# Attention keys in three full chunks and a shared rest, in a fused attention and SwiGLU kernel

## The chip, the cores and the metric

The kernel runs on one core of a Trainium2 chip. The metric is device time in microseconds (us), lower is better. The kernel before takes 453.81 us (median of three runs, 453.68 to 455.35). In the profiled execution the span from the first to the last instruction is 451.7 us, with a mean granted TensorE clock of 0.998. "PE" is TensorE, "PEld" its weight loads, "DVE" VectorE, "ACT" ScalarE, "POOL" GpSimd, "SP" SyncE.

## What is computed

Softmax attention over 8 batches and 12 heads, 448 tokens, head size 64; its output, with the heads side by side, is the input of a SwiGLU block with widths 768, 1536 and 768.

```python
batch, n_heads, seq, head_dim = (8, 12, 448, 64)
scores = scale * np.matmul(q, k.transpose(0, 1, 3, 2))
attn = softmax(scores)                       # over the keys
attn_out = np.matmul(attn, v)
x = attn_out.transpose(0, 2, 1, 3).reshape(3584, 768)
g = x @ w_gate                               # 768 x 1536
val = x @ w_val                              # 768 x 1536
return (silu(g) * val) @ w_out               # 1536 x 768
```

(Shortened: the reference subtracts the row maximum before the exponential; the names are its own.)

## The kernel before

The heads are worked in 48 pairs. For each pair the keys stand as four chunks of 112. `qk` computes the scores of one chunk for both heads (two matmuls, each on 64 rows of the array) and ScalarE takes their exponential into E. PV multiplies E with V and a column of ones (65 columns), and VectorE closes the pair: a reciprocal of the sums and a multiplication. The result is transposed into X. The FFN takes X in blocks of 384 or 512 tokens. Its first part has twelve steps per block: a gate group of six matmuls (gp), a value group of six (vp), tanh on ScalarE (sg), and two operations on VectorE (t, hts). Its second part has output steps of twelve matmuls (op), each copied by ScalarE to osb and sent out.

```python
ps_s = ctx.enter_context(tc.tile_pool(name="ps_s", bufs=3, space=PSUM))   # [128, 2, 512] each
ps_f = ctx.enter_context(tc.tile_pool(name="ps_f", bufs=2, space=PSUM))   # one bank each
...
def qk(pr, c):
    s = ps_s.tile([128, 2, 512], FP32, tag="s")
    for hx in range(2):
        nc.tensor.matmul(s[:, hx, 0:S], lhsT=t[ts(hx, 64), c * P : c * P + 128], rhs=..., ...)
    nc.scalar.activation(e[:, :, 0:S], s[0:P, :, 0:S], AF.Exp, scale=sm_scale)
...
def pv_chunk(pr, c):
    if c == 0:
        accs[pr] = ps_f.tile([128, 512], FP32, tag="f", name="acc")
    ...                                      # 8 matmuls of 65 columns, both heads in one bank
    nc.vector.reciprocal(r[:, 0:7], a7[:, :, D])
    nc.vector.tensor_tensor(xt[:, 0:n], a7[:, 0:n, 0:D], r[...], ALU.mult)
...
def ffn1_steps(kk, c0, n, hts):
    for fb in range(NFB):
        ...
        gp = ps_s.tile([128, 2, 512], FP32, tag="s", name="gp")[:, 0]     # or a ps_f tile
        group("g", gp)
        nc.scalar.activation(sg[:, 0:n], gp[:, 0:n], AF.Tanh, scale=0.5)
        vp = ps_f.tile([128, 512], FP32, tag="f", name="vp")
        group("v", vp)
        nc.vector.scalar_tensor_tensor(t1[:, 0:n], sg[:, 0:n], 1.0, gp[:, 0:n], ALU.add, ALU.mult)
        nc.vector.scalar_tensor_tensor(hts[:, fb, 0:n], t1[:, 0:n], 0.5 * HS, vp[:, 0:n], ...)
        yield
...
def ffn2_steps(...):
        op = ps_f.tile([128, 512], FP32, tag="f")
        for fb in range(NFB):
            nc.tensor.matmul(op[:, 0:w], lhsT=hts[:, fb, ts(ch, 128)], rhs=wo[oh][...], ...)
        nc.scalar.activation(osb[:, ds(m0, w)], op[:, 0:w], AF.Copy, scale=1.0 / HS)
        ...                                  # DMA to out
```

The order is fixed by the program. After an opening of attention alone it goes in visits: two or three score chunks of later pairs, the PV of a ripe pair if there is one (a visit without is called bare), then steps of the FFN.

Of the kernel before, what the change touches and what calls it, by code (L numbers as in the profile page):

```python
# [26 lines left out]
NX = 6  # L27
NV = 5
VS = 9
EB = 15  # L30
# [3 lines left out]
def kernel(  # L34
# [24 lines left out]
    MQ = S - D  # L59
# [13 lines left out]
    load_table("exp_and_others")  # L73

# [7 lines left out]
    ps_f = ctx.enter_context(tc.tile_pool(name="ps_f", bufs=2, space=PSUM))  # L82

    Es = [consts.tile([P, NC * EB + 1, D], FP16, name=f"E{i}") for i in range(NE)]
    Xts = [consts.tile([128, 7, D], FP16, name=f"xt{i}") for i in range(NX)]
    Xrs = [consts.tile([D, 128], FP16, name=f"xr{i}") for i in range(3)]
    Vts = [consts.tile([P, 2, NC, D + 2], FP16, name=f"vo{i}") for i in range(NV)]
    vraw = consts.tile([P, VS, 2, NC, D], FP16, name="vraw")
# [17 lines left out]
    def dummy(n):  # L106
        wp = ps_f.tile([128, 512], FP32, tag="f", name="wp")
        for _ in range(n):
            nc.tensor.matmul(wp[:], lhsT=warm[:, 0:128], rhs=warm[:], start=True, stop=True)  # L109

    def load_qk32(pr):
        rq = raws.tile([P, 2, NC, D], FP32, tag="rq", bufs=RB)
        rk = raws.tile([P, 2, NC, D], FP32, tag="rk", bufs=RB)
        for dst, src in ((rq, q), (rk, k)):
            nc.sync.dma_start(dst[:], src[0, 2 * pr : 2 * pr + 2].rearrange("h (p c) d -> p h (c d)", c=NC))
        raw[pr] = (rq[:], rk[:])
# [3 lines left out]
    def load_qk16(pr, n=2):  # L120
        h0 = 2 * (pr % 2) if pr >= 14 else 0
        if h0 == 0:
            q16 = raws.tile([P, 4, NC, D], FP16, tag="rq", bufs=RB, name="q16")
            k16 = raws.tile([P, 4, NC, D], FP16, tag="rk", bufs=RB, name="k16")
            pairbuf[:] = [q16, k16]
        q16, k16 = pairbuf
        for dst, src in ((q16, q), (k16, k)):
            flat = src.rearrange("b h s d -> (b h) s d")[2 * pr : 2 * pr + 2 * n]
            nc.gpsimd.dma_start(dst[:, ds(h0, 2 * n)], flat.rearrange("h (p c) d -> p h (c d)", c=NC))  # L129
        for i in range(n):  # L130
            h = h0 + 2 * i
            raw[pr + i] = (q16[:, h : h + 2], k16[:, h : h + 2])

    def load_v(pr, n=1):
        b, h = divmod(2 * pr, H)
        nc.gpsimd.dma_start(  # L136
            vraw[:, ds(pr % VS, n)].rearrange("p r h c d -> p (r h) (c d)"),
            v[b, h : h + 2 * n].rearrange("h (p c) d -> p h (c d)", c=NC),
        )
# [17 lines left out]
    def prep(pr):  # L157
        rq, rk = raw[pr]
        if pr == 0 or pr >= NPE:
            qk16 = attp.tile([P, 2, NC, 2, D], FP16, tag="qk16", bufs=3)  # L160
            for t, src in enumerate((rq, rk)):
                dst = qk16[:, 1 - t].rearrange("p c h d -> p h c d")
                if pr == 0:
                    nc.vector.tensor_copy(dst[:, 0], src[:, 0])
                    nc.scalar.activation(dst[:, 1], src[:, 1], AF.Copy)
                else:
                    nc.gpsimd.tensor_copy(dst, src)  # L167
        qkT[pr] = attp.tile([128, 2 * S + D], FP16, tag="qkT", name="qkT", bufs=5)
        if pr >= NPE:
            nc.sync.dma_start_transpose(  # L170
                qkT[pr][:, 0 : 2 * S].rearrange("p (c q) -> p c q", q=P),
                qk16[:].rearrange("p t c h d -> p (t c h d)"),
            )
            nc.sync.dma_start_transpose(
                qkT[pr][:, 2 * S :].rearrange("p (c q) -> p c q", c=1),
                qk16[0:D, 1, 0].rearrange("p h d -> p (h d)"),
            )
            return None

        def turn0():  # L180
            for t in range(2):
                tp = ps_s.tile([128, 2, 512], FP32, tag="s", name="tp")
                for c in range(NC):
                    for hx in range(2):
                        nc.tensor.matmul(
                            tp[ts(hx, 64), c // 2, ds(c % 2 * P, P)],
                            lhsT=qk16[:, 1 - t, c, hx],
                            rhs=ident[0:P, 0:P],
                            start=True,
                            stop=True,  # L190
                        )
                dst = qkT[pr][:, ts(1 - t, S)].rearrange("p (a x) -> p a x", a=2)
                nc.vector.tensor_copy(dst[:, 0], tp[:, 0, 0 : 2 * P])
                nc.scalar.activation(dst[:, 1], tp[:, 1, 0 : 2 * P], AF.Copy)
                if t == 0:
                    tq = tp
            nc.vector.tensor_copy(qkT[pr][:, 2 * S :], tq[:, 0, 0:D])

        def turn():
            if pr < FIRST + 2:  # L200
                tp = ps_s.tile([128, 2, 1024], FP16, tag="s", name="tp")[:, 0]
            else:
                tp = ps_f.tile([128, 1024], FP16, tag="f", name="tp")
            for i in range(2 * NC + 1):
                t, c = (1 - i // NC, i % NC) if i < 2 * NC else (0, 0)
                for hx in range(2):
                    src = raw[pr][t][:, hx, c, :]
                    nc.tensor.transpose(tp[ts(hx, 64), ts(i, P)], src, ident[0:P, 0:P])  # L208
            nc.vector.tensor_copy(qkT[pr][:], tp[:, 0 : 2 * S + D])  # L209
# [3 lines left out]
    def qk(pr, c):  # L213
        t = qkT[pr]
        s = ps_s.tile([128, 2, 512], FP32, tag="s")
        for hx in range(2):
            nc.tensor.matmul(  # L217
                s[:, hx, 0:S],
                lhsT=t[ts(hx, 64), c * P : c * P + 128],
                rhs=t[ts(hx, 64), ds(S + (1 - hx) * D, S)],  # L220
                start=True,
                stop=True,
            )
        e = Es[pr % NE][:, ds(c * EB, 16)].rearrange("p (h b) x -> p h (b x)", h=2)
        nc.scalar.activation(e[:, :, 0:S], s[0:P, :, 0:S], AF.Exp, scale=sm_scale)  # L225

    def qk_half(pr, half, between=None):
        for c in (2 * half, 2 * half + 1):
            qk(pr, c)
            if between and c % 2 == 0:  # L230
                between()
# [3 lines left out]
    def pv_chunk(pr, c):  # L235
        if c == 0:
            accs[pr] = ps_f.tile([128, 512], FP32, tag="f", name="acc")
        e = Es[pr % NE]
        vo = Vts[pr % NV]
        a7 = accs[pr][:, 0 : 7 * (D + 1)].rearrange("p (s d) -> p s d", s=7)  # L240
        for j in range(3):
            for hx in range(2):
                nc.tensor.matmul(  # L243
                    a7[:, 2 * j + hx],
                    lhsT=e[:, ds(c * EB + 9 * hx + 2 * j, 2)].rearrange("p b x -> p (b x)"),
                    rhs=vo[:, hx, c, 0 : D + 1],
                    start=c + j + hx == 0,
                    stop=False,
                )
        for hx in range(2):  # L250
            nc.tensor.matmul(  # L251
                a7[:, 6],
                lhsT=e[:, ds(c * EB + 6 + hx, 2)].rearrange("p b x -> p (b x)"),
                rhs=vo[:, hx, c, 0 : D + 1],
                start=False,
                stop=c == NC - 1 and hx == 1,
            )
        if c < NC - 1:
            return
        r = attp.tile([128, 8], FP32, tag="R", bufs=2, name="R")  # L260
        xt = Xts[pr % NX]
        nc.vector.reciprocal(r[:, 0:7], a7[:, :, D])  # L262
        n = 7 if pr < XPE else 6
        nc.vector.tensor_tensor(  # L264
            xt[:, 0:n],
            a7[:, 0:n, 0:D],
            r[:, 0:n].unsqueeze(2).to_broadcast([128, n, D]),
            ALU.mult,
        )
        if pr < XPE:  # L270
            return
        for hx in range(2):
            nc.vector.tensor_scalar(
                Xrs[pr % 3][:, ts(hx, D)], a7[ts(hx, D), 6, 0:D], r[ts(hx, D), 6:7], None, ALU.mult
            )

    def pv(pr):
        for c in range(NC):
            pv_chunk(pr, c)

    def turn_x(pr):
# [5 lines left out]
        xt = Xts[pr % NX]  # L287
        if pr < XPE:
            tp = accs[pr] if pr < FIRST else ps_f.tile([128, 512], FP32, tag="f", name="xtp")
            for j in range(3):  # L290
                nc.tensor.matmul(  # L291
                    tp[:, ts(j, 128)],
                    lhsT=xt[:, 2 * j : 2 * j + 2].rearrange("p h d -> p (h d)"),
                    rhs=ident[:],
# [3 lines left out]
            nc.vector.tensor_copy(dst[:, 0:MQ], tp[:, 0:MQ])  # L298
            return
        nc.sync.dma_start_transpose(  # L300
            dst[:, 0:MQ].rearrange("p (j q) -> p j q", j=3),
            xt[:, 0:6].rearrange("p j d -> p (j d)"),
        )
        nc.sync.dma_start_transpose(dst[:, MQ:S].rearrange("p (j q) -> p j q", j=1), Xrs[pr % 3][:])

    def turn_rests(b):
        tp = ps_f.tile([128, NHP, D], FP32, tag="f", name="rtp")
# [334 lines left out]
```

The softmax here doesn't subtract the row's maximum and nothing guards it: scores larger than these inputs give would overflow.

## Time and profile before

| what | before |
|---|---|
| time, median of 3 | 453.81 us |
| span of the profiled execution | 451.7 us |
| VectorE, ScalarE, POOL busy | 45%, 53%, 31% |
| exponentials | 192, mean 919 ns |
| first gate group of the FFN starts | 29.79 us |
| last score and PV work | before 386 us, then FFN alone |

A busy share is an average over stages. Matmuls are pipelined and the ends that the profile gives them are modelled, so a rate is read from the distance of two starts. In a line of the timeline the columns are start, length, engine, source line, operation, out<-in, shape and count; in brackets stands the idle time of that engine ahead of it and what ended it.

### The profile page before, as it was taken

What the parts mean: (1) busy time and instruction counts of PE and PEld (TensorE: products, weight loads), DVE (VectorE), ACT (ScalarE), POOL (GpSimd) and SP (SyncE); (2) the same over time, 40 slices, a digit from 0 to 9 for tenths busy, and PEclk for the clock granted to TensorE, in tenths of its full rate; (3) what the DMA queues carried; (4) which work ended last, traced back from release to release, by engine and by line L of the source; (5) the groups of instructions that cost most, each with busy time, mean ns of one, the idle gap of its engine ahead of it and who ended that gap; (6) DMA issues with size and microseconds to landing.
All of it is one profiled execution on the core that took longest, in us unless ns stands there. A gap on an engine that the chain in (4) does not pass through costs nothing.

```text
span 451.7 us, 9871 instructions
## 1 busy us (share of the span) xinstructions
PE 441.9 (98%) x4024; PEld 247.0 (55%) x4024; DVE 201.6 (45%) x447; ACT 238.8 (53%) x350; POOL 141.8 (31%) x228
## 2 busy tenths in 40 slices
PE   8999999999999999999999999999999999999995
PEld 3655565545455556454555656545455666544563
DVE  3666562456654434455443534353453544055300
ACT  6965666566746465554554546644555462222221
POOL 8755715927642225252313405330100000000000
PEclk9999999999999999999999999999999999999999
DMA  9999999999969379874749758772503112200033
GB/s 142 173 200 201 196 172 174 180 209 119 145 93 133 46 129 124 132 120 71 126 74 120 98 78 143 118 105 68 101 20 68 46 46 57 70 2 0 17 100 95
DMA packets 105101, 48.71 MB, mean 108 GB/s; under 512 B 59744, under 2 KB 101600, under 8 KB 105056
## 3 DMA queue, kind: packets, MB, share of 16 engines
q0 software_dynamic: 43392, 23.37, 41.2%
q1 hardware_dynamic: 61664, 24.71, 28.9%
q8 instruction: 31, 0.51, 0.5%
q14 instruction: 14, 0.11, 0.1%
HBM read 47.19 MB, written 11.01 MB: 129 GB/s over the span
## 4 chain that ended last, share of the span: by engine, by line
PE 93%; DVE 3%; ACT 2%; issue 1%; DVEq 0%; ACTq 0%
PE op L371 24%; PE gp L326 23%; PE vp L326 23%; PE s L217 9%; PE acc L243 9%; PE acc L251 2%; ACT E L225 2%; PE tp L208 1%; PE wp L109 1%; DVE t L345 1%; ACT sg L341 1%; DVE qkT L209 0%; DVE xt L264 0%; PE acc L291 0%; DVE hts L348 0%
## 5 line engine op out<-in xcount | busy, mean ns | idle before, releaser
L225 ACT ACTIVATE E<-s 112x896 f16<-112x896 f32 x192 | 162.1, 919 | 27.5 <-PE s L217 27.4
L326 PE MATMUL gp<-X,wg 128*128 128x384 f16 (+1 forms) x576 | 124.7, 352 | 0.0
L326 PE MATMUL vp<-X,wv 128*128 128x384 f16 (+1 forms) x576 | 124.6, 352 | 0.0
L371 PE MATMUL op<-wo,hts 128*128 128x384 f16 (+1 forms) x684 | 116.1, 323 | 0.0
L345 DVE SCALAR_TENSOR_TENSOR t<-sg,gp 128x384 f32<-128x384 f32 (+1 forms) x96 | 59.7, 621 | 121.8 <-ACT sg L341 121.8
L341 ACT ACTIVATE sg<-gp 128x384 f32<-128x384 f32 (+1 forms) x96 | 52.5, 547 | 84.8 <-PE gp L326 83.6
L371 PEld LDWEIGHTS <-hts 128*128 128x128 f16 x684 | 65.5, 98 | 45.9 <-issue 3.9
L326 PEld LDWEIGHTS <-wv 128*128 128x128 f16 x576 | 56.3, 98 | 52.6
L326 PEld LDWEIGHTS <-wg 128*128 128x128 f16 x576 | 53.1, 97 | 45.6 <-issue 1.1
L378 ACT ACTIVATE osb<-op 128x384 f32<-128x384 f32 (+1 forms) x57 | 27.8, 487 | 92.5 <-PE op L371 92.5
L167 POOL COPY qk<-q 112x512 f16<-112x512 f16 x37 | 22.9, 619 | 144.5 <-DMA qkT<-qk 143.1
L348 DVE SCALAR_TENSOR_TENSOR hts<-t,vp 128x384 f16<-128x384 f32 (+1 forms) x96 | 59.6, 621 | 10.0
L243 PEld LDWEIGHTS <-E 112*128 112x128 f16 x1152 | 46.7, 97 | 18.2 <-issue 17.5
L243 PE MATMUL acc<-vo,E 112*128 112x65 f16 x1152 | 53.0, 193 | 1.3 <-DVE vo L142 0.7
L217 PE MATMUL s<-qkT 64*128 64x448 f16 x384 | 50.6, 355 | 0.2
L251 PE MATMUL acc<-vo,E 112*128 112x65 f16 x384 | 42.9, 193 | 0.0
L262 DVE RECIPROCAL R<-acc 128x7 f32<-128x7 f32 x48 | 9.8, 205 | 70.6 <-PE acc L251 70.5
L129 POOL DMA_DIRECT2D k<-in_k_dram x44 | 29.0, 660 | 9.5 <-DMA wo<-in_moe_w_out_dram 7.8
L129 POOL DMA_DIRECT2D q<-in_q_dram x44 | 29.3, 666 | 5.2 <-PE s L217 2.5
L136 POOL DMA_DIRECT2D vraw<-in_v_dram x42 | 28.0, 666 | 8.4 <-DVE vo L142 7.2
L217 PEld LDWEIGHTS <-qkT 64*128 64x128 f16 x384 | 14.5, 94 | 25.8 <-issue 18.6
L264 DVE TENSOR_TENSOR xt<-acc,R 128x384 f16<-128x384 f32 (+1 forms) x48 | 27.6, 574 | 1.7
(41 smaller groups left out, 148.2 us busy)
## 6 DMA issues: line engine op xcount, KB each, us to landing
q<-in_q_dram POOLq DMA_DIRECT2D x41, 112.0 KB, 4.0
k<-in_k_dram POOLq DMA_DIRECT2D x41, 112.0 KB, 4.6
vraw<-in_v_dram POOLq DMA_DIRECT2D x39, 112.0 KB, 4.6
wg<-in_moe_w_gate_dram POOLq DMA_DIRECT2D x8, 288.0 KB, 10.1
wv<-in_moe_w_val_dram POOLq DMA_DIRECT2D x8, 288.0 KB, 10.2
wo<-in_moe_w_out_dram POOLq DMA_DIRECT2D x2, 1152.0 KB, 22.0
out_dram<-osb SPq DMA_DIRECT2D x8, 288.0 KB, 3.0
out_dram<-osb SPq DMA_DIRECT2D x8, 240.0 KB, 3.1
```

Source lines behind the costliest of these rows:

```text
L129: nc.gpsimd.dma_start(dst[:, ds(h0, 2 * n)], flat.rearrange("h (p c) d -> p h (c d)", c=NC))
L136: nc.gpsimd.dma_start(vraw[:, ds(pr % VS, n)].rearrange("p r h c d -> p (r h) (c d)"), v[b, h : h + 2 * n].rearrange("h (p c) d -> p h (c ...
L217: nc.tensor.matmul(s[:, hx, 0:S], lhsT=t[ts(hx, 64), c * P : c * P + 128], rhs=t[ts(hx, 64), ds(S + (1 - hx) * D, S)], start=True, stop=True,)
L225: nc.scalar.activation(e[:, :, 0:S], s[0:P, :, 0:S], AF.Exp, scale=sm_scale)
L243: nc.tensor.matmul(a7[:, 2 * j + hx], lhsT=e[:, ds(c * EB + 9 * hx + 2 * j, 2)].rearrange("p b x -> p (b x)"), rhs=vo[:, hx, c, 0 : D + 1] ...
L251: nc.tensor.matmul(a7[:, 6], lhsT=e[:, ds(c * EB + 6 + hx, 2)].rearrange("p b x -> p (b x)"), rhs=vo[:, hx, c, 0 : D + 1], start=False, st ...
L326: nc.tensor.matmul(dst[:, 0:n], lhsT=wslice(kind, fb, cb), rhs=X[kk][:, cb, ds(c0, n)], start=(cb == 0), stop=(cb == NCB - 1),)
L341: nc.scalar.activation(sg[:, 0:n], gp[:, 0:n], AF.Tanh, scale=0.5)
L345: nc.vector.scalar_tensor_tensor(t1[:, 0:n], sg[:, 0:n], 1.0, gp[:, 0:n], ALU.add, ALU.mult)
L348: nc.vector.scalar_tensor_tensor(hts[:, fb, 0:n], t1[:, 0:n], 0.5 * HS, vp[:, 0:n], ALU.mult, ALU.mult)
L371: nc.tensor.matmul(op[:, 0:w], lhsT=hts[:, fb, ts(ch, 128)], rhs=wo[oh][:, fb, ds(m0 - oh * OH, w)], start=(fb == 0), stop=(fb == NFB - 1),)
L378: nc.scalar.activation(osb[:, ds(m0, w)], op[:, 0:w], AF.Copy, scale=1.0 / HS)
```

## The change

Keys are split into three chunks of 128 and a rest of 64 instead of four chunks of 112. The rests of the four heads of two neighbouring pairs share one score tile: four matmuls on 64x64 quarters of the array, and one exponential. This is meant to fill the array's and ScalarE's 128 lanes. Keys of pairs up to 10 are loaded with seven tokens per partition and split by transposes on TensorE. V, and the keys of later pairs, are loaded in two halves of 64 partitions that share a token row. Each head's PV now has a PSUM bank of its own. The PSUM pool of two tiles becomes one tile F with two banks, and a helper hands out its halves in turn. The mix of FFN steps in a visit is planned anew so that a visit, where it can, ends with an output step. Some loads move (wo later, pair 0's q on ScalarE's queue).

```diff
+    ps_f = ctx.enter_context(tc.tile_pool(name="ps_f", bufs=1, space=PSUM))
+    F = ps_f.tile([128, 2, 512], FP32, name="F")
+    fturn = [0]
+
+    def fbank():
+        fturn[0] ^= 1
+        return F[:, 1 - fturn[0]]
...
+    def load_keys(eng, dst, src, h0, n):
+        for s in range(2):
+            rows = bass.AP(
+                src.tensor, (h0 * S + s * KR) * D, [[(2 * NC - 1) * D, 64], [S * D, n], [1, NC * D]]
+            )
+            eng.dma_start(dst[ts(s, 64)], rows)
...
     def qk(pr, c):
-        t = qkT[pr]
         s = ps_s.tile([128, 2, 512], FP32, tag="s")
+        if c < KR:
+            t = qkT[pr]
             for hx in range(2):
                 nc.tensor.matmul(
+                    s[:, hx, 0:S],
+                    lhsT=t[ts(hx, 64), ts(c + low(pr, hx), 128)],
...
+        else:
+            for hx in range(2):
+                for p in (pr, pr + 1):
+                    lo = low(p, hx)
+                    t = qkT[p]
+                    nc.tensor.matmul(
+                        s[ts(1 - lo, 64), hx, 0:S],
+                        lhsT=t[ts(hx, 64), ds(0 if lo else KR * 128 + 64, 64)],
...
+    def pv_open(pr):
+        if pr not in accs:
+            accs[pr] = ([F[:, 0], F[:, 1]] if pr < FIRST else [fbank(), fbank()], [0, 0])
...
+    def pv_close(pr):
+        ...
         for hx in range(2):
+            a4 = accs[pr][0][hx][:, 0 : (KR + 1) * (D + 1)].rearrange("p (s d) -> p s d", s=KR + 1)
+            nc.vector.reciprocal(r[:], a4[:, :, D])
+            nc.vector.tensor_tensor(xt[:, :, hx], a4[:, :, 0:D], r[...], ALU.mult)
...
             if gate_small[0]:
-                gp = ps_f.tile([128, 512], FP32, tag="f", name="gp")
+                gp = fbank()
...
-            vp = ps_f.tile([128, 512], FP32, tag="f", name="vp")
+            vp = fbank()
...
-                op = ps_f.tile([128, 512], FP32, tag="f")
+                op = fbank()
...
+            no = [int(x + y + 1 < len(plan) and bool(plan[x + y + 1][1])) for y in range(visits)]
...
+                for _ in range(nf):
+                    run_fv()
                 for _ in range(no):
                     run_o()
```

(Cut to its core; the diff as a whole also changes the opening's order and the layout of E, V and the transposes.)

## The prediction

> **What bounds the kernel now.** I read the page's busy shares and its chain first, then the costliest groups, then the timeline of one steady visit and of the tail.
>
> ```profile
> PE 441.9 (98%) x4024; PEld 247.0 (55%) x4024; DVE 201.6 (45%) x447; ACT 238.8 (53%) x350; POOL 141.8 (31%) x228
> PE 93%; DVE 3%; ACT 2%; issue 1%; DVEq 0%; ACTq 0%
> L371 PE MATMUL op<-wo,hts 128*128 128x384 f16 (+1 forms) x684 | 116.1, 323 | 0.0
> L378 ACT ACTIVATE osb<-op 128x384 f32<-128x384 f32 (+1 forms) x57 | 27.8, 487 | 92.5 <-PE op L371 92.5
> L264 DVE TENSOR_TENSOR xt<-acc,R 128x384 f16<-128x384 f32 (+1 forms) x48 | 27.6, 574 | 1.7
> ```
>
> TensorE is the bound: busy 98%, 93% of the chain, and its output step (op) waits for nothing. ScalarE's copy of that step waits 92.5 us for TensorE, never the reverse. What hides the copies shows in the timeline of one visit:
>
> ```profile
> 142.44 0.74 PE L217 MATMUL s<-qkT 64*128 64x448 f16 x6
> 142.84 2.53 ACT L225 ACTIVATE E<-s 112x896 f16<-112x896 f32 x3 [0.78 <-PE s L217]
> 143.11 0.36 PE L243 MATMUL acc<-vo,E 112*128 112x65 f16 x6
> ...
> 144.09 1.14 PE L326 MATMUL gp<-X,wg 128*128 128x384 f16 x6
> 144.29 0.20 DVE L262 RECIPROCAL R<-acc 128x7 f32<-128x7 f32 x1 [0.78 <-PE acc L251]
> ...
> 147.01 1.14 PE L326 MATMUL vp<-X,wv 128*128 128x384 f16 x6
> 147.21 0.49 ACT L341 ACTIVATE sg<-gp 128x384 f32<-128x384 f32 x1 [1.46 <-PE gp L326]
> 147.74 0.56 DVE L345 SCALAR_TENSOR_TENSOR t<-sg,gp 128x384 f32<-128x384 f32 x1 [0.73 <-ACT sg L341]
> ...
> 147.99 2.11 PE L371 MATMUL op<-wo,hts 128*128 128x384 f16 x12
> ...
> 148.40 0.56 DVE L348 SCALAR_TENSOR_TENSOR hts<-t,vp 128x384 f16<-128x384 f32 x1
> ...
> 150.03 0.74 PE L217 MATMUL s<-qkT 64*128 64x448 f16 x6
> 150.14 0.49 ACT L378 ACTIVATE osb<-op 128x384 f32<-128x384 f32 x1 [2.43 <-PE op L371]
> ```
>
> Steps between starts give TensorE's rates: gate or value group 0.975 us (1.295 at 512 columns, from 423.62 to 424.91 in the tail), output step 1.95, a PV matmul 0.030 (32 of them from 143.11 to 144.09), a score chunk 0.19 (three in 0.67, less 0.10). About 0.1 us is lost on entering the scores and again on leaving them. The value group ends at 147.985 and the output step starts at 147.99, although hts reads that value bank until 148.96. It can, because the two have different tiles. The tail shows the same without attention, a copy (0.49) every 1.9 to 2.0 us behind steps of 1.95:
>
> ```profile
> 438.76 0.49 ACT L378 ACTIVATE osb<-op 128x384 f32<-128x384 f32 x1 [1.41 <-PE op L371]
> 440.76 0.49 ACT L378 ACTIVATE osb<-op 128x384 f32<-128x384 f32 x1 [1.51 <-PE op L371]
> 442.66 0.49 ACT L378 ACTIVATE osb<-op 128x384 f32<-128x384 f32 x1 [1.41 <-PE op L371]
> ```
>
> **What the Trainium skill says.** "TensorE: Matmul & The Clock Gate", Part 3, says row and column tiles of the array run together. The trace agrees: two 448-column score matmuls cost 0.19 us[...]. "TensorEngine Tiling (Array Packing)", Key Properties, says that changing the mode drains the array; those are the two losses of 0.1. "PSUM — Partial Sum Buffer", the section on bank collisions, asks for guards by bank and quadrant: an engine reading one bank does not forbid TensorE another. The lines at 147.99 and 148.40 agree. "Perfetto Trace Analysis", Optimization Strategy, takes one repeated gap on the engine that should be saturated as a sign of too few PSUM buffers; the kernel before has none in the steady part, but I expect them after.
>
> **What the change saves.** (1) Scores: 192 chunks become 144 chunks and 24 shared rests. If four 64x64 tiles run together, a rest is 0.19 too: 24 x 0.19 = 4.5 us. (2) PV: still 1,536 matmuls, but 384 of them use half the rows in pairs: 192 x 0.030 = 5.7 us. (3) Mode changes: counted in the two instruction orders, 172 become 185, +1.3. Pure TensorE work, summed at these rates with the unchanged FFN (327 us), transposes and 2.6 of warm-up, goes from 436.0 to 427.1 us. (4) In the opening ScalarE is the limit: 26 exponentials before the first FFN group become 23, and 0.84 us each (2.53/3) makes 2.5 us. Before, TensorE starts at 1.2 and loses some 9 us to waits, 5.6 of them ahead of its first FFN group at 29.79; its matmuls end near 446.5.
>
> **What it adds: waits.** This decides my number. PSUM for accumulators, value groups, output steps and X transposes was a pool of two tiles. Now it is one tile F of two banks, from which a helper hands out alternate halves. In the built changed program the semaphore values show each user of F waiting for the reader of the *previous* user, although that reads the other bank:
>
> ```
> PE op -> F at 512: waits Activation >= 314, set by the copy of the op just before, at F offset 0
> PE op -> F at 0:   waits Activation >= 315, set by the copy of the op just before, at F offset 512
> ```
>
> In the program before, the same step waits for the copy of two steps earlier. So dependences are kept for F as a whole: two banks, but a depth of one. I counted these waits in the built program and priced each kind. Latencies from the visit: PE stream end to ACT or DVE 0.20 us; ACT to DVE 0.03; t end to hts 0.10; back to PE about 0.06 (the one short wait in the opening: xt ends 29.56, TensorE starts 29.61).
>
> - Output step after output step, 17 times: 0.20 + 0.49 (copy) + 0.06 = 0.75. Sum 12.6 (the last piece is shorter).
> - Output step after a value group, 40 times: hts must end. Counted from the gate group's end at 384: tanh to 0.69, t to 1.28, hts from 1.39 to 1.95, TensorE 2.01; the value group took 0.975 of it, so 1.04 is lost; 1.09 at 512 columns (operations of 0.60, 0.69, 0.69). In six bare visits (no PV, the gate in F) t also waits for the value group: 1.46 or 1.74. Sum 18 x 1.04 + 16 x 1.09 + 3 x 1.46 + 3 x 1.74 = 45.8.
> - Value group after PV, 42 times: both heads' close must end. 0.20, two reciprocals of 0.2 and two multiplies of 256 columns (0.44 each, from 0.56 at 384 and 0.62 at 448), gaps 0.1, 0.06: 1.64 after PV, less a gate group and 0.03. 25 x 0.64 + 17 x 0.32 = 21.4.
> - Value group after a gate in F, 10 times: tanh must be over, and stands behind the visit's three exponentials. Those end 3.0 to 3.2 us into the visit and tanh 0.5 to 0.6 later, while the gate ended at 1.8 or 2.4: 1.9 at 384 (3 times), 1.3 at 512 (3), and 4.2 for the four in the first block. Sum 13.9.
> - X transposes after a value group, 6 x 1.04 = 6.2.
> - PV after a copy, value after value, gate after copy: these have 0.66 us or more of other work between, and cost 0 to 0.3 each: together 5.
>
> The sum is 105 us, all of it on TensorE, which is the path. In all: 1.2 start + 427.1 + 5 of opening waits + 105 + 1 small ones = 539; then 5.2 from the last matmul to the end of the span as before, and 2.1 from span (451.7) to time (453.81): 546 us.
>
> **Rivals.** *A: the chip runs the two banks independently, and only the savings count.* The matmul rates speak for these; the result would be 453.8 - 8.9 - 1 to 2.5 = 442 to 444 us. Against it stand the wait values, which are instructions in the program and not a guess at the hardware. *B: the waits are as counted but mostly hidden,* because ScalarE and VectorE start sooner than I take them to, or TensorE has other work in the way: half the sum, 490 to 500 us. Against it: the order on TensorE has the waiting group directly after its predecessor at all 57 output steps, with nothing between to fill the gap. *C: the DMA supply binds.* The page has the DMA engines at nine tenths or more in the first ten slices (113 us), V (and K from pair 11) are now loaded with 64 of 448 rows twice, and each V load takes two POOL issues of 0.66 us. This could cost 1 to 4 us in the opening, but a TensorE slowed by 20% asks for data later, so afterwards the queues get slack. *D: the 64x64 rests or the half-row PV matmuls don't overlap:* +4.5 and +5.7 us on top of mine.
>
> **Range and chances.** The count of the waits is fixed; the uncertain part is their price (0.1 us on each of 105 is 10 us) and the opening (3 us either way). Low side: 526, if waits are 20% cheaper; high side: 562, with D and dearer restarts. Slower by over 2% at 0.97; the rest is for A.
>
> **What would show it.** TensorE's busy share near 84% instead of 98%, and new idle time. The profile's modelled end of a matmul covers 0.16 us of each wait (147.99 + 2.11 is 150.10, the stream ends at 149.94), so it would show ahead of op about 39 us released by DVE hts and 10 by ACT osb, ahead of vp about 15 by DVE xt and 12 by ACT sg. In the tail, output steps every 2.7 us instead of 1.95. Exponentials 168 instead of 192, of the same length. Against me: output steps at 1.95 in the tail, or a span under 500; then F is not one dependence. If rests take 0.38 us or the eight half-row PV matmuls 0.24, step (1) or (2) is wrong.

## The result, and the profile after

The changed kernel takes 549.1 us (median of four runs, 547.0 to 550.1) against 453.75 us before: 1.209 times as long, with a 95% interval of 1.204 to 1.214. The prediction was 546 us with a range of 526 to 562. In the profiled execution the span is 547.7 us at a mean granted clock of 0.994, against 451.7 and 0.998.

The page of the kernel after. First line: busy time and share of the span of each engine. Then the rows of the groups (busy us, mean ns of one | idle before, releaser) that answer to those shown of the kernel before. (The chain of this page reaches back only to 379.5 us, so its shares don't compare with those before.)

```profile
PE 459.7 (84%) x4080; PEld 248.3 (45%) x4080; DVE 202.0 (37%) x459; ACT 218.9 (40%) x326; POOL 183.8 (34%) x306
L427 PE MATMUL F<-wo,hts 128*128 128x384 f16 (+1 forms) x684 | 120.0, 325 | 48.8 <-DVE hts L404 38.9
L382 PE MATMUL F<-X,wv 128*128 128x384 f16 (+1 forms) x576 | 124.7, 352 | 20.7 <-ACT sg L397 11.0
L434 ACT ACTIVATE osb<-F 128x384 f32<-128x384 f32 (+1 forms) x57 | 27.7, 486 | 188.9 <-PE F L427 188.9
```

TensorE fell from 98% busy to 84%, and an output step that waited for nothing before now stands behind 48.8 us of idle time. The instructions themselves are as long as before: a matmul of an output step takes 325 ns in the mean (323 before), a copy 486 (487). ScalarE still waits for TensorE ahead of its copies, and longer than before, 188.9 us against 92.5. So the two engines now wait for each other in turn, as one shared dependence would have it. The waits of TensorE (us in total, times, longest):

```profile
PE F L427 <- DVE hts L404: 38.9, 40, 1.6
PE F L382 <- ACT sg L397: 11.0, 10, 1.5
PE F L427 <- ACT osb L434: 9.8, 17, 0.6
PE F L382 <- DVE xt L330: 8.8, 24, 0.7
PE F L358 <- DVE hts L404: 3.9, 6, 0.6
PE F L295 <- DVE xt L319: 3.0, 3, 1.4
```

Every one of them is a user of F that waits for the reader of F before it. One visit in the timeline (start, us, then the instruction and the idle time before it) shows where they sit:

```profile
176.29 1.14 PE L382 MATMUL gp<-X,wg 128*128 128x384 f16 x6
176.56 0.18 DVE L329 RECIPROCAL R<-F 128x4 f32<-128x4 f32 x1 [3.98 <-PE F L295]
...
177.33 0.42 DVE L330 TENSOR_TENSOR xt<-F,R 128x256 f16<-128x256 f32 x1
...
177.81 1.14 PE L382 MATMUL F<-X,wv 128*128 128x384 f16 x6 [0.38 <-DVE xt L330]
...
179.75 1.14 PE L382 MATMUL F<-X,wv 128*128 128x384 f16 x6
...
181.20 0.55 DVE L404 SCALAR_TENSOR_TENSOR hts<-t,F 128x384 f16<-128x384 f32 x1
...
181.80 2.11 PE L427 MATMUL F<-wo,hts 128*128 128x384 f16 x12 [0.91 <-DVE hts L404]
```

The output step starts at 181.80, 0.05 us after hts has ended (181.20 + 0.55), and not at the end of the value group's stream at 180.72 (179.75 + 0.975). In the kernel before the same step started 0.4 us *before* hts did. The tail, without attention:

```profile
514.62 2.11 PE L427 MATMUL F<-wo,hts 128*128 128x384 f16 x12 [0.91 <-DVE hts L404]
...
516.77 0.49 ACT L434 ACTIVATE osb<-F 128x384 f32<-128x384 f32 x1 [3.71 <-PE F L427]
...
517.31 2.11 PE L427 MATMUL F<-wo,hts 128*128 128x384 f16 x12 [0.58 <-ACT osb L434]
```

An output step every 2.69 us where it was 1.95: the copy (0.49) and its two handovers are no longer hidden.

### The profile page after: what moved, and what is told of

It reads as the page before. It is cut to its first block, busy times and chain, and to the rows that moved or that the text cites. A ratio compares the mean times of both kernels' runs of the same rounds, so it can differ in the third digit from the quotient of the medians.

```text
span 547.7 us, 10122 instructions
## 1 busy us (share of the span) xinstructions
PE 459.7 (84%) x4080; PEld 248.3 (45%) x4080; DVE 202.0 (37%) x459; ACT 218.9 (40%) x326; POOL 183.8 (34%) x306
## 5 line engine op out<-in xcount | busy, mean ns | idle before, releaser
L427 PE MATMUL F<-wo,hts 128*128 128x384 f16 (+1 forms) x684 | 120.0, 325 | 48.8 <-DVE hts L404 38.9
L382 PE MATMUL F<-X,wv 128*128 128x384 f16 (+1 forms) x576 | 124.7, 352 | 20.7 <-ACT sg L397 11.0
L281 ACT ACTIVATE E<-s 128x896 f16<-128x896 f32 x144 | 123.1, 922 | 20.6 <-PE s L260 20.5
L382 PE MATMUL gp<-X,wg 128*128 128x512 f16 (+1 forms) x516 | 112.3, 354 | 0.0
L434 ACT ACTIVATE osb<-F 128x384 f32<-128x384 f32 (+1 forms) x57 | 27.7, 486 | 188.9 <-PE F L427 188.9
L397 ACT ACTIVATE sg<-gp 128x512 f32<-128x512 f32 (+1 forms) x86 | 47.4, 551 | 97.4 <-PE gp L382 95.8
L401 DVE SCALAR_TENSOR_TENSOR t<-sg,gp 128x512 f32<-128x512 f32 (+1 forms) x86 | 53.7, 624 | 86.2 <-ACT sg L397 86.1
L404 DVE SCALAR_TENSOR_TENSOR hts<-t,F 128x384 f16<-128x384 f32 (+1 forms) x96 | 59.6, 621 | 15.8 <-PE F L382 8.6
L295 PE MATMUL F<-vo,E 128*128 128x65 f16 x1152 | 44.9, 193 | 1.8 <-DVE vo L169 1.1
L295 PEld LDWEIGHTS <-E 128*128 128x128 f16 x1152 | 38.4, 97 | 5.6 <-issue 3.2
L330 DVE TENSOR_TENSOR xt<-F,R 128x256 f16<-128x256 f32 x84 | 35.7, 425 | 3.2 <-DVE R L329 0.3
```

What stands on the lines that cost most here:

```text
L281: nc.scalar.activation(e[:, 0 : 2 * S].rearrange("p (h q) -> p h q", h=2), s[:, :, 0:S], AF.Exp, scale=sm_scale)
L295: nc.tensor.matmul(accs[pr][0][hx][:, ts(j, D + 1)], lhsT=e[rows, ds(hx * S + j * 128, 128)], rhs=Vts[pr % NV][rows, hx, col, 0 : D + 1], ...
L330: nc.vector.tensor_tensor(xt[:, :, hx], a4[:, :, 0:D], r[:].unsqueeze(2).to_broadcast([128, KR + 1, D]), ALU.mult,)
L382: nc.tensor.matmul(dst[:, 0:n], lhsT=wslice(kind, fb, cb), rhs=X[kk][:, cb, ds(c0, n)], start=(cb == 0), stop=(cb == NCB - 1),)
```

## The experiments

The theory: F as one dependence makes nearly all of the loss. Rivals for the loss: the new instructions themselves (rests and half-row PV that don't overlap), the order of the visits, and the supply of data. All kernels below compute the whole reference.

### Two tiles in place of one, and the reverse

In the changed kernel, F becomes two tiles of one bank each, and the close of a pair in the opening, which read both banks with one operation, reads them one after the other. Nothing else is changed.

```diff
-    F = ps_f.tile([128, 2, 512], FP32, name="F")
+    F = [ps_f.tile([128, 512], FP32, name=f"F{i}") for i in range(2)]
 ...
-        return F[:, 1 - fturn[0]]
+        return F[1 - fturn[0]][:]
```

> The changed kernel with F as two tiles of one bank each instead of one tile of two banks; nothing else, except that the opening closes each head by itself (four VectorE operations per pair instead of two). Theory (dependence on F as a whole): the waits of 105 us shrink to those a bank really needs (bare visits 8 us, first block 3 to 4, a few more), so 455 to 463 us, and output steps in the tail every 1.95 us. Rival (the new order, more and smaller loads or half-filled matmul modes cost the time, the waits only show it): above 500 us.

Measured: 469.89 us, 1.035 times before (1.032 to 1.038). The tail's output steps come every 1.95 us again (144 matmuls in 21.64 us). The reverse: the kernel *before* with its pool of two tiles replaced by one tile handed out in halves (its late transposes of q and k, a third kind of user, go to the score pool).

```diff
-    ps_f = ctx.enter_context(tc.tile_pool(name="ps_f", bufs=2, space=PSUM))
+    ps_f = ctx.enter_context(tc.tile_pool(name="ps_f", bufs=1, space=PSUM))
+    F = ps_f.tile([128, 2, 512], FP32, name="F")
 ...
-                op = ps_f.tile([128, 512], FP32, tag="f")
+                op = fbank()          # F[:, 0] and F[:, 1] in turn; so too acc, vp, gp, xtp, rtp
```

> The kernel before with its pool of two PSUM tiles replaced by one tile of two banks handed out in turn (its late transposes go to the score pool, because the tile holds another type); attention, plan and loads as before. Theory: the one-tile dependence alone brings some 85 us, 520 to 550 us, with output steps in the tail every 2.7 us. Rival (the loss belongs to the new attention or plan): within 10 us of the kernel before.

Measured: 550.51 us, 1.213 times before (1.211 to 1.216). The waits of TensorE in it:

```profile
PE F L374 <- DVE hts L351: 21.8, 27, 1.0
PE F L374 <- ACT osb L381: 9.6, 17, 0.6
PE F L329 <- DVE xr L276: 8.0, 18, 0.5
```

The dependence, on the old chunks, the old order and the old loads, costs 97 us, and taking it away from the changed kernel gives back 79 of its 95 us. The same kinds of waits appear, 17 times the copy among them. That is the cause of most of the loss, shown from both sides. Not all of the 97 us are waits: from 26.4 to 46.7 us this kernel ran at a granted clock of 0.50, busy for 15.4 us, so up to some 8 us went to the clock (an estimate: half of the busy time). That the old chunks (550.5 us) and the new (549.1) are level with one tile therefore doesn't say what the rest of the change is worth: it has other waits in other places, and with two tiles the rest costs 17 us.

What I missed: I expected 455 to 463 us with two tiles. The kernel lay 17 us above the one before, and the next runs ask for these. (The reverse came 0.5 us above the 520 to 550 that I expected.)

### Output step first in bare visits

The change ends each visit with its output step. In a visit without PV, gate, value group and output step then crowd on the two banks. In the two-tile kernel TensorE waits there:

```profile
PE F L416 <- DVE t L390: 5.5, 6, 1.1
```

This kernel is the two-tile kernel with the gate always in the score pool and, in bare visits, the output step ahead of the FFN's first part.

```diff
-                gate_small[0] = bare
+                gate_small[0] = False
+                if bare and no:
+                    run_o()
+                    no -= 1
                 for _ in range(nf):
                     run_fv()
```

> Two tiles as in e1_two_tiles, and in bare visits the gate group goes to the score pool and the output step comes first. Theory: an output step behind a gate in F waits 1.0 to 1.6 us for tanh and t in six or seven visits; so 5 to 9 us below e1_two_tiles, about 450 us. Rival (those waits are covered by something else that is late too): the same as e1_two_tiles within 2 us.

Measured: 464.35 us, 1.024 times before (1.022 to 1.026). That wait is gone. The 5.5 us under the two-tile kernel are as expected, the level (450) isn't: what remained was more than I had counted.

### An earlier opening

In the output-first kernel, V of pairs 3 to 5 is loaded ahead of q and k of pair 5; in the opening V is prepared and PV issued ahead of the transposes of q and k, and the last X transposes take a bank of F.

```diff
-        load_qk16(5, 1)
         load_v(3, GP)
+        load_qk16(5, 1)
 ...
         for u in range(NU0):
             qk(pr, c)
+            if u in CAT: copy_v(CAT[u])
+            for _ in range(2): ...            # PV pieces, moved up from behind the transposes
             if u in TAT: ...
```

> As e2_output_first, and in the opening V of pairs 3 to 5 is loaded ahead of q and k of pair 5, PV and close stand ahead of the transposes of a step, and the last X transposes use a free bank of F. Theory: the opening loses time on VectorE, where a close stands behind other copies, and on V that lands late; the first FFN group comes 2 to 4 us earlier than in e2_output_first, the time falls by as much. Rival (ScalarE's exponentials or the banks set the opening): no change within 1 us.

Measured: 464.52 us, 1.024 times before (1.022 to 1.026). The first FFN group came at 32.39 us in place of 34.17, and the end did not move. The waits of TensorE say why:

```profile
PE s L273 <- DMA qkT<-qk: 4.5, 1, 4.5
PE s L260 <- DMA qkT<-qk: 2.8, 1, 2.8
```

In the kernel with the late opening these two were 1.8 and 2.4. TensorE reaches the keys of pairs 12 and later earlier, by 0.7 and 1.9 us, and they are not there: it goes on at 79.14 and 87.22 us, with the late opening at 79.38 and 86.47. Time gained ahead of a late transfer is waited away. GpSimd's timeline in the output-first kernel shows what holds them up:

```profile
53.53 1.04 POOL L182 DMA_DIRECT2D wo<-in_moe_w_out_dram  x1 [2.17 <-issue]
...
59.29 1.06 POOL L182 DMA_DIRECT2D wo<-in_moe_w_out_dram  x1
...
66.55 0.60 POOL L123 DMA_DIRECT2D k<-in_k_dram  x1 [4.44 <-DMA wo<-in_moe_w_out_dram]
...
76.57 0.59 POOL L123 DMA_DIRECT2D k<-in_k_dram  x1 [4.87 <-DMA wo<-in_moe_w_out_dram]
```

Two issues of keys stand over 4 us each behind a load of half the output weights (1.15 MB): each waits for the eighth load before it, the first for the one issued at 53.53, the second for the one at 59.29. And the wait is not the whole loss. The clock around the two waits of the output-first kernel (stretch, length, busy time of PE, PEld, DVE, ACT and POOL with instructions, granted clock, DMA share, GB/s):

```profile
77.30:80.70 3.40, 1.32 (x35) 1.16 (x36) 1.08 (x4) 2.16 (x3) 2.68 (x5) 0.99 1.19 150
80.75:84.10 3.35, 3.35 (x12) 1.51 (x10) 1.34 (x4) 0.49 (x1) 3.35 (x7) 0.51 1.20 118
84.15:87.50 3.35, 1.51 (x21) 0.69 (x20) 0.93 (x2) 0.60 (x1) 3.35 (x7) 1.00 1.35 149
87.55:90.90 3.35, 3.35 (x30) 1.98 (x28) 1.21 (x4) 1.88 (x3) 3.35 (x7) 0.50 1.32 148
```

After each of the two waits the granted clock is half for some 3.4 us: TensorE works slowly just when it has to catch up. The Trainium skill, "TensorE: Matmul & The Clock Gate", Part 1, says the clock is gated down to half after an idle window of about 3.4 us. The trace agrees on the half, but not on the idle window: the single waits were 2.4 and 1.8 us, and in the 3.4 us before each fall TensorE was still busy for 1.32 and 1.51 us.

### The output weights in small loads

The kernel with the earlier opening and eight loads of 288 KB, spread over pairs 9 to 14; and the same loads with the change's own opening.

```diff
-            8: [("o", 0)],
-            9: [("o", 1)],
+            9: [("o", 0, 0)],
+            10: [("o", 0, 1)],
+            11: [("o", 0, 2)],
+            12: [("o", 0, 3)],
+            13: [("o", 1, 0), ("o", 1, 1)],
+            14: [("o", 1, 2), ("o", 1, 3)],
```

> e3_opening with the output weights in eight loads of 288 KB spread over pairs 9 to 14, in place of two of 1.15 MB at pairs 8 and 9. Theory: what the two-tile kernels lack against the kernel before is the supply of keys around 75 to 90 us: GpSimd, which issues the loads and waits for the eighth before, is held 4.4 and 4.9 us behind the two large loads, the keys of pairs 12 and 13 come late, TensorE waits 2.8 and 4.5 us for their transposes, and its clock falls afterwards. With small loads the two waits fall below 1 us each and no 5 us slice at 80 to 95 us has a clock under 0.95: 454 to 458 us. Rival: the bytes themselves are too many by then, whatever their order; the waits move to another pair: 462 to 466 us.

> e2_output_first with the same eight loads, and the opening as the change has it. If the supply theory holds, the 1.8 us that e3_opening gained by its opening are now seen at the end: this is 1 to 2.5 us above e4_wo_spread, at 456 to 460 us. If the supply still binds, the two are the same, as e2 and e3 were.

Measured: 457.34 us, 1.0085 times before (1.007 to 1.010), and 458.33 us, 1.0106 (1.0089 to 1.0123). Both waits for transposed keys are gone, and the clock is 1.00 in every stretch from 75 to 100 us. With the change's own opening the small loads brought 6.0 us (464.35 to 458.33): two waits of 4.2 us together, and two stretches of 3.4 us at half clock. So it was the order and size of the loads, and not the sum of bytes. The 1.0 us between the two kernels has the sign that I expected of the opening, but the two intervals overlap, and in these profiles its first FFN group comes no earlier (34.10 us, with the change's own opening 33.49), so I don't credit it with that. One reason is in the profile: in it TensorE still ran slowly at 9.39 us, where the same pair of score matmuls ran fast at 8.14 in the kernel with that opening and the large loads:

```profile
9.39 0.56 PE L260 MATMUL s<-qkT 64*128 64x448 f16 x2
```

```profile
8.14 0.36 PE L260 MATMUL s<-qkT 64*128 64x448 f16 x2
```

### The opening head by head

In the changed kernel each pair of the opening holds both banks until its close. This kernel, made from the one with the earlier opening and small loads, works all pieces of one head, closes it, then the other.

```diff
-            pieces += [(p, c) for c in (...)]
+            pieces += [(p, c, hx) for hx in range(2) for c in (...)]
 ...
-            p, c = pieces.pop(0)
-            pv_piece(p, c)
+            p, c, hx = pieces.pop(0)
+            pv_piece(p, c, (hx,))          # and pv_close(p, (hx,)) after the head's last piece
```

> e4_wo_spread with PV in the opening (pairs 0 to 5) head by head: all pieces of one head, its close, then the other head, in place of both heads piece by piece and both closes at the end. Theory: the opening is late because each pair holds both banks until it is closed, so that TensorE waits for xt (2.2 us in e4_wo_spread before 33 us, and 1.3 us for the last X transposes); with one bank per head in turn the waits for xt by PV fall to 0.5 us or less, the first FFN group comes 1 to 2 us earlier than in e4_wo_spread, and the end moves by the same: 455 to 456.5 us. Rival: TensorE only follows the exponentials and the loads of V in the opening; then the waits move to vo or to the scores' buffers and the time stays at 457 to 458 us.

Measured: 459.75 us, 1.015 times before (1.013 to 1.016): slower than the kernel it came from, though the first FFN group starts at 29.65 us, 0.1 us ahead of the kernel before. Of the 34.10 us in the kernel it came from, part was the clock; the fair comparison is with the 32.39 of the first kernel with that opening, and the gain 2.7 us, more than the 1 to 2 that I had expected. The waits up to 34 us, first two lines from the kernel it came from, then this one:

```profile
PE F L295 <- DVE xt L319: 2.2, 5, 0.8
ACT E L281 <- PE s L260: 7.1, 8, 1.6
```

```profile
ACT E L281 <- PE s L260: 2.7, 5, 1.0
```

The cause of the late opening is thus shown: PV's waits for xt went to nothing, and with them most of what ScalarE waited for scores (5.5 us in the first kernel with that opening). But a new wait took it all back. Timeline:

```profile
57.69 0.29 DVE L169 COPY vo<-vraw 128x512 f16<-128x512 f16 x1 [6.08 <-DMA vraw<-in_v_dram]
...
58.58 1.76 PE L371 MATMUL F<-X,wv 128*128 128x384 f16 x5 [4.63 <-DVE xt L319]
```

The releaser named for TensorE is a close on VectorE, yet VectorE only stood behind its copy of V of pair 9, whose load had not landed. After the wait the clock was 0.50 from 57.2 to 63.9 us.

### Loads in the order of need

In the head-by-head kernel, the loads of V for pairs 9 to 11 and of q and k for pairs 12 and 13 go ahead of the last quarter of the gate and value weights. The second kernel also begins the transposes of keys four pairs ahead, not three, with six buffers; the third also gives xt five buffers, not three.

```diff
-            4: [("g", 3), ("v", 3), ("qk", 12)],
-            6: [("V", 3)],
+            4: [("V", 3), ("qk", 12), ("g", 3), ("v", 3)],
```

```diff
-                if NPE <= pr + 3 < NPAIR:
-                    prep(pr + 3)
+                if NPE <= pr + 4 < NPAIR:
+                    prep(pr + 4)
```

```diff
-NX = 3
+NX = 5
```

> e6_head_by_head with the loads of V for pairs 9 to 11 and of q and k for pairs 12 and 13 moved ahead of the last quarter of the gate and value weights, which is first needed some 20 us later. Theory: e6's opening starts the FFN at 29.65 us, 4.4 us earlier than e4, and loses it at 54 us, where VectorE stands 6.1 us in the copy of V of pair 9, whose load has not landed, with the close of pair 8 behind it; TensorE waits 4.6 us for that close and its clock falls to 0.80 to 0.86 for some 20 us. With V in time both go: 452 to 455 us, level with the kernel before. Rival: the loads up to 60 us are more bytes than the queue can bring by then in any order; the wait moves to the gate or value weights or to the keys of pair 12: 457 to 460 us.

> e7_v_first with the casts and transposes of a pair's keys begun four pairs ahead in place of three, and six buffers in place of five for them. Theory: what is left of the supply loss in e7 is one wait of 2.4 us at 70 us for the transposed keys of pair 15, which the shared rest needs a pair earlier than its own scores do, and a clock of 0.83 for 10 us after it (1.7 us). Begun one pair earlier both go: 452 to 453.5 us, level with the kernel before or 0.2% under it. Rival: the casts then stand in GpSimd's order ahead of loads that are as urgent, and the wait moves to a load of V or of the output weights: 456 to 458 us.

> e8_keys_earlier with five buffers for xt in place of three. Theory: the last single wait above 1 us after the opening in e8 is at 96 us, 1.8 us, a close of PV that stands 2.75 us because its buffer xt is still being transposed to X. With two more buffers it goes: 452 to 453 us, level with the kernel before or up to 0.3% under it. Rival: the transposes themselves are late, and then the FFN waits for X or the keys instead: 454 us as e8.

Measured: 456.61 us (1.0070, 1.0048 to 1.0091), then 454.35 us (1.0023, 1.0008 to 1.0038), then 453.45 us against 453.41 (1.0002, 0.9987 to 1.0017). Each removed the wait it was built against. The first two left another behind, 2.4 us for the keys of pair 15 and 1.8 us for a buffer of xt, and lie 1.6 and 0.9 us above what was expected; the last lies 0.5 above, and is level with the kernel before. (The intervals of the last two overlap, so that the 0.9 us between them is not shown.) TensorE's waits in it, beside those of the kernel before:

```profile
PE F L295 <- DVE hts L393: 2.4, 7, 0.6
PE F L116 <- DVE warm L453: 1.2, 1, 1.2
PE F L295 <- DVE X L354: 1.0, 3, 0.3
PE F L347 <- DVE xt L319: 0.9, 1, 0.9
```

```profile
PE wp L109 <- DVE warm L407: 1.2, 1, 1.2
PE acc L291 <- DVE xt L264: 1.0, 1, 1.0
PE acc L243 <- DVE vo L142: 0.7, 1, 0.7
```

Where did the gain of the shared rest go? I summed, over TensorE's whole timeline, the time from each start to the next less the idle time shown: 442.3 us of work and 2.8 idle before, 438.5 and 7.9 in the last kernel. The change saves 3.7 us of TensorE's work, and 5.1 us of short waits stand against it. In 3.4 us of the 7.9, PV of a visit waits for the hts or X copy before it; that two banks per pair make these waits is my reading, which no run tests. So TensorE's last matmul even ends 1.3 us later than before (447.87 us against 446.55). The spans are level only because this one ends 3.3 us after its last matmul and not 5.2. There the last stores of the output go out on two queues (SyncE's and ScalarE's), before on SyncE's alone; that this is the reason is not tested. No version here is faster than the kernel before.

## Why the prediction was right

**F as one dependence** carried the number, and it held. From the timeline after, as the distance between starts less the group's own time:

- Output step after a value group, 40 times: 45.5 us, predicted 45.8.
- Output step after output step: 0.74 us for each full one, predicted 0.75.
- Value group after a gate in F, 10 times: 13.6, predicted 13.9.
- X transposes after a value group, 6 times: 4.8, predicted 6.2.
- Value group after PV, 42 times: 16.5, predicted 21.4. This term was mis-sized: the two closes took 1.19 us (176.56 to 177.75), not the 1.38 in my sum, and began 0.27 us after PV and not 0.20, so some 0.53 and 0.21 us were lost each time where I had 0.64 and 0.32. Of the idle time shown, that is 8.8 us against about 15.

**Steps 1 to 3, the savings,** were put at 8.9 us together. By the same timeline sums, scores fell from 46.4 to 42.4 us and PV from 48.6 to 47.4: 5.2. Of the 42.4, 1.5 us are again waits for F: 22 times PV stands behind the scores of a visit and starts only 0.05 us after the copy has ended (175.32, the copy at 174.78 + 0.49). It is the wait "PV after a copy", too short to show as idle time, so the savings were 6.7 us; why not 8.9 I can't say.

The tiles do overlap, as I said they would: the score chunk after a rest starts 0.32 us behind it (183.84 to 184.16, with a mode change of 0.1 in it), not 0.38 and more, and eight half-row PV matmuls take 0.12 to 0.13 where score matmuls in the same mode follow. For scale, one matmul of 448 columns would take 0.19 alone at a gate group's rate (an estimate: 0.975/6 x 448/384), as long as two of them did. But where full-row PV follows, as in nearly all visits, the eight take 0.21 to 0.24, which is what eight full-row matmuls took before (8 x 0.030). By my own test ("the eight half-row PV matmuls 0.24") step 2 is wrong there, though not for lack of overlap: the 0.1 us of the mode change, which before stood behind the scores, now stands behind the half-row pair (the count of mode changes is the predicted 185). So rival D is out for the rests; for PV its cost came true, its cause did not.

**Step 4, the opening,** was wrong in sign. The three fewer exponentials were to bring 2.5 us; the first FFN group came at 33.85 us, 4.1 later than before. I took ScalarE for the limit there. It waited 7.2 us for scores in the first 34 us, against 1.1 before, because TensorE stood in front of the banks of the pair before. The head-by-head kernel shows it: the same exponentials, and the group at 29.65. Part of the 4.1 us is the clock here too: in this profile a pair of score matmuls still took 0.56 us at 9.35, before it took 0.36 at 9.21. But the change's own opening came at 33.49 and 34.17 us also in the two-tile kernels whose clock was up early.

The total is nearer than its terms. The five waits listed came to 7.0 us less than predicted and the end after the last matmul to 1.9 less (3.3 us, not 5.2); the savings fell 2.2 us short, the opening came 6.6 later, and an output step at half clock (3.71 us in place of 2.04, at 316.99), which no term had, added 1.7. That is 8.9 us one way and 10.5 the other; that 546 lay only 3.1 us from 549.1 is in part luck. The 9 us of waits that the prediction gives the kernel before were a remainder too: its timeline shows 2.8 us of idle time after the start and 442.3 us of work, not 436.0.

**Rival A** (only the savings count) and **B** (half hidden) fall with the tail at 2.69 us, the waits above and the 79 and 97 us of the two exchanges. **Rival C**, supply, did not show in the changed kernel: none of TensorE's waits there names a DMA. It was there all the same, hidden behind the 100 us. With two tiles the large loads of output weights cost 6.0 us, and the opening's gain of some 4 us could be kept only once V and keys were loaded in time.

## What to carry to other kernels

Count the tiles that rotate and not the banks: two banks handed out from one tile were one dependence here, and that cost 97 us of 454. The Trainium skill, "Perfetto Trace Analysis", Optimizing Tensor Performance, asks that matmul groups rotate through different banks so that evacuation overlaps the next group; these kernels all rotate, and only with a tile for each bank did it overlap. When a large wait is taken away, look next at the loads that it had given time to: order them by when they are first needed, and keep a long one from standing ahead of a short and urgent one.

## What the runs showed that I had not expected

- Single waits of TensorE of 1.8 to 2.5 us were followed by some 3.4 us at a granted clock of 0.50, so that a wait cost more than its length: the small loads took away 4.2 us of waits for keys (1.8 and 2.4) and brought 6.0 us. Many short waits were followed by it too: the one-tile kernel with the old chunks, with no single wait above 0.7 us in the 8 us before, ran at 0.50 from 26.4 to 46.7 us.
- Half-row matmuls of 65 columns in pairs came at 15 to 17 ns each (eight in 0.12 to 0.13 us), but with full-row matmuls behind them the eight took 0.21 to 0.24.
- A releaser on VectorE can stand for a DMA: a close that ran late stood behind a copy that waited 6.1 us for its load.
